# An attention-and-feed-forward layer on one core: query, key and value projections in nine 64-row blocks instead of five 128-row ones

## The chip, the core and the metric

The kernel runs on one core of one Trainium2 chip. The metric is device time in microseconds (us). Three runs of the kernel before the change took 446.04, 446.70 and 447.26 us; their median is 446.7 us. Profiles come from one execution each. A difference below about 0.3% (1.3 us) can't be told from no change here.

## What is computed

x has 2048 tokens of 576 features, in bf16. The attention cuts the tokens into four segments of 512. Within a segment it is ordinary causal attention with 32 heads of 18 features; across segments a memory matrix M and a vector z are carried on. A feed-forward of width 4608 follows.

```python
q, k, v = ln(x) @ wq, ln(x) @ wk, ln(x) @ wv          # 576 x 576 each
for s in range(4):                                    # segments of 512 tokens
    a_dot = softmax(qs @ ks.T * scale + causal mask) @ vs
    a_mem = phi(qs) @ M / (phi(qs) @ z + 1e-6)        # phi(t) = t + 1 if t > 0 else exp(t)
    o = g * a_mem + (1 - g) * a_dot
    M, z = M + phi(ks).T @ vs, z + sum(phi(ks))
h   = x + o @ wo
out = h + gelu(ln(h) @ w1 + b1) @ w2 + b2             # 576 -> 4608 -> 576
```

## The kernel before

The work is cut by segment and, inside one, by tile of 128 tokens. `stage_X` (line 752) normalizes the four x tiles of a segment and brings them into `xreg` with the features on the partitions. `stage_P` (line 845) multiplies them by wk, wq and wv, tile by tile. `stage_A0` and `stage_A` (lines 969 and 1104) do the attention of segment 0 and of segments 1 to 3, `stage_M` (line 915) updates the memory, `stage_B` (line 1224) multiplies by wo, adds x and normalizes again, and `stage_C` (line 1273) does the feed-forward: first product at lines 1337 (segment 0) and 1300, second at 1387.

**Projections.** 576 features are four blocks of 128 rows and one of 64. x is stored 640 wide: its last 64 features stand twice, so that the fifth block holds them in both halves of the partitions. The weights of the fifth block have the 64 rows in the upper half for the first 288 output columns and in the lower half for the others, and zeros elsewhere. One projection of one tile has three forms:

- `proj2` (line 830, matmuls at 837): 10 matmuls over all 128 rows. k and q of the first two tiles of segment 0 use it.
- `proj_pair` fused (line 823): also 10 matmuls over 128 rows, five for each of the two PSUM banks.
- `proj_pair` in two pieces (line 797): 18 matmuls over 64 rows, two at a time in the two halves of the array, 10 in the first piece and 8 in the second. Each half of the rows writes one bank in the first piece and the other bank in the second. Between them VectorE or GpSimd does a tiny memset (`pass`, line 803), which the second piece waits for.

The output projection with wo uses `proj_pair` as well. The first product of the feed-forward (lines 1300 and 1337) has a form of its own: nine blocks of 64 rows, each half of the array with its own bank from beginning to end, and a `by_pair` layout of the weights that gives the two halves the nine blocks in different orders.

**Turning x.** In segment 0 five TensorE transposes a tile (`TX`, line 747) fill a PSUM bank, and one copy on ScalarE or VectorE (lines 643 and 647) takes all five blocks into `xreg`. In segments 1 to 3 the tiles are stored to DRAM (`xnd`), and one transposing DMA for each pair of tiles (line 634, queue of SyncE) brings five blocks of 256 columns back.

**Start.** Eight matmuls on zeros (`warm_up`, line 657) and two more (line 661) run while the first x tile arrives. Its first half comes over SyncE's queue, its second half and the whole second tile over ScalarE's queue (lines 685 and 687); the two halves of the k weights follow on SyncE's queue. Three more zero matmuls stand behind the first tile's transposes, and the first projection waits for them.

**Buffers.** `xreg` has 19 blocks of 512 columns: two slots of five for x, and two of nine for the feed-forward's input, one of which lies over the first. PSUM is eight banks; a score takes four (`st`), a projection two. `t1` (two buffers) holds the values after the transposition of a group's result from PSUM (lines 1047 and 1196) until `comb` (1056) or `comb2` (1207) has read them. Five `pt` tiles hold exponentiated scores.

**Order.** Nothing is scheduled by the hardware or by a framework. `TIMETABLE` gives each operation a rank and an engine; `Graph.schedule` sorts by rank and emits each engine's instructions in that order. Each engine works through its own list strictly in order, so an instruction that waits holds up all behind it.

The functions that the change touches, and what calls them:

Of the kernel before, what the change touches and what calls it, by code (L numbers as in the profile page):

```python
# [13 lines left out]
F32 = mybir.dt.float32  # L14
BF16 = mybir.dt.bfloat16
# [458 lines left out]
def kernel(  # L474
# [11 lines left out]
    nc = tc.nc  # L486
# [1062 lines left out]
```

## Time and profile before

| | |
|---|---|
| runs | 446.04, 446.70, 447.26 us, median 446.7 |
| profiled execution | 446.14 us; span from first to last instruction 444.4 us |
| granted TensorE clock | 1.000 |
| TensorE busy | 433.7 us (98%) |
| VectorE, ScalarE, GpSimd busy | 286.3, 298.1, 179.5 us |
| DMA | 76.26 MB, 63.5% of 16 engines' time on the main queue |

How to read it: a matmul's end is modelled in the profile and covers its way through the array, so neighbouring matmuls overlap. Start-to-start distances and merged pieces of the chain say more than the mean of one. The chain of waits is the sequence of work that ended last, followed back from the end; where it runs through one engine without a break, that engine sets the time.

### The profile page before, as it was taken

To read this page: it belongs to the slowest core of one execution; us is meant where nothing else is said; L and a number is where in the kernel's file an instruction comes from. 1 tells how busy PE (TensorE), PEld (TensorE's weight loads), DVE (VectorE), ACT (ScalarE), POOL (GpSimd) and SP (SyncE) were. 2 spreads that over 40 slices of the span, in tenths; PEclk is the share of its full clock that TensorE was granted. 3 is DMA by queue.
4 is the path that set the end of the run, shared out by engine and by line. 5 is a ranking of instruction groups with operands and counts; after the bars stand their busy time and mean duration, and the time that the engine had idled before them with its cause. 6 is when DMAs were issued, how large, how long until landed. Compare 5 with 4: busy or idle time off the path is not lost.

```text
span 444.4 us, 12086 instructions
## 1 busy us (share of the span) xinstructions
PE 433.7 (98%) x5089; PEld 277.8 (63%) x5089; DVE 286.3 (64%) x635; ACT 298.1 (67%) x274; POOL 179.5 (40%) x321
## 2 busy tenths in 40 slices
PE   8978999999999999999999999999999999999997
PEld 4755677776677676664444766654457775446775
DVE  4899988899778998968788888642875410000011
ACT  3799889999878898776799976675855001565000
POOL 4587657356735765834132765412111400110000
DMA  7599989997999955893783236913634357550110
GB/s 283 167 217 258 257 251 283 251 287 203 191 270 333 286 118 175 175 236 94 162 228 91 73 90 193 232 20 133 219 97 165 90 142 133 172 177 1 40 41 29
DMA packets 81591, 76.26 MB, mean 172 GB/s; under 512 B 59008, under 2 KB 68864, under 8 KB 81536
## 3 DMA queue, kind: packets, MB, share of 16 engines
q1 hardware_dynamic: 81248, 75.23, 63.5%
q8 instruction: 40, 0.66, 0.6%
q10 hardware_dynamic: 288, 0.25, 0.2%
q14 instruction: 15, 0.12, 0.1%
HBM read 42.30 MB, written 19.20 MB: 138 GB/s over the span
## 4 chain that ended last, share of the span: by engine, by line
PE 87%; DVE 5%; ACT 4%; DMA 2%; issue 1%; ACTq 0%; SPq 0%; DVEq 0%
PE bank L1387 32%; PE bank L1300 24%; PE bank L1337 7%; PE bank L797 6%; PE bank L823 5%; PE bank L1162 4%; PE bank L1188 3%; ACT pt L1166 1%; PE bank L837 1%; DMA x<-in_A_x_dram 1%; DMA beta_bc<-in_A_beta_dram 1%; PE bank L1133 1%; PE bank L1001 1%; ACT pt L1004 1%; DVE pt L1014 1%
## 5 line engine op out<-in xcount | busy, mean ns | idle before, releaser
L1166 ACT ACTIVATE pt<-bank 128x2048 bf16<-128x2048 f32 x60 | 112.6, 1876 | 29.5 <-PE bank L1162 23.2
L1387 PEld LDWEIGHTS <-hT 128*128 128x128 bf16 x1152 | 110.2, 98 | 34.5 <-issue 6.7
L1300 PE MATMUL bank<-xreg,w1g 64*128 64x512 bf16 x972 | 108.0, 376 | 0.0
L1300 PEld LDWEIGHTS <-w1g 64*128 64x128 bf16 x972 | 46.5, 94 | 57.4 <-issue 3.7
L1387 PE MATMUL bank<-w_lo,hT 128*128 128x288 bf16 x576 | 78.1, 286 | 0.0
L1387 PE MATMUL bank<-w,hT 128*128 128x288 bf16 x576 | 77.4, 286 | 0.0
L1399 DVE TENSOR_TENSOR ot<-bank,hc 128x288 bf16<-128x288 f32 x32 | 13.8, 448 | 88.4 <-PE bank L1387 72.5
L1177 POOL TENSOR_SCALAR_AFFINE_SELECT pt<-pt 128x512 bf16<-128x512 bf16 x64 | 45.0, 717 | 42.5 <-ACT pt L1166 41.6
L1305 ACT ACTIVATE hT<-bank,b_col 128x512 bf16<-128x512 f32 x36 | 22.2, 695 | 46.5 <-PE bank L1300 46.3
L1315 DVE TENSOR_SCALAR hT<-bank,b_col 128x512 bf16<-128x512 f32 x46 | 32.8, 741 | 22.1 <-PE bank L1300 20.4
L1373 POOL TENSOR_TENSOR hc<-hc,b_bc 128x576 f32<-128x576 f32 x9 | 11.8, 1320 | 79.0 <-DMA hc<-hd 79.0
L1004 ACT ACTIVATE pt<-bank 128x2048 bf16<-128x2048 f32 x20 | 37.4, 1876 | 4.1 <-PE bank L1001 2.9
L1337 PE MATMUL bank<-xreg,w1g 64*128 64x256 bf16 x648 | 38.1, 269 | 0.0
L823 PE MATMUL bank<-hT,xreg 128*128 128x288 bf16 x250 | 33.8, 286 | 1.7 <-ACT pt L1004 1.0
L1337 PEld LDWEIGHTS <-w1g 64*128 64x128 bf16 x648 | 30.4, 94 | 6.6 <-issue 3.2
L1320 ACT ACTIVATE hT<-hT 128x8192 bf16<-128x8192 bf16 (+2 forms) x6 | 31.8, 5323 | 0.1
L823 PEld LDWEIGHTS <-xreg 128*128 128x128 bf16 x250 | 23.4, 98 | 10.0 <-issue 4.3
L1313 ACT ACTIVATE hT<-bank,b_col 128x512 bf16<-128x512 f32 x26 | 16.9, 685 | 16.1 <-PE bank L1300 15.8
L797 PE MATMUL bank<-hT,xreg 64*128 64x288 bf16 x342 | 24.9, 283 | 0.9 <-DVE qk_pad L647 0.7
L1204 POOL TENSOR_TENSOR t<-t,r 128x288 f32<-128x288 f32 x17 | 13.6, 802 | 29.2 <-DVE r L1201 29.2
L1348 DVE TENSOR_TENSOR hT<-bank,b_col 128x512 bf16<-128x512 f32 x31 | 20.4, 682 | 6.0 <-PE bank L1337 5.8
L1162 PE MATMUL bank<-qk 32*128 32x512 bf16 (+3 forms) x384 | 23.8, 301 | 0.2
(120 smaller groups left out, 592.1 us busy)
## 6 DMA issues: line engine op xcount, KB each, us to landing
w1g<-in_B_w_dram SPq DMA_DIRECT2D x41, 576.0 KB, 5.0
qkd<-qk_pad SPq DMA_DIRECT2D x15, 512.0 KB, 4.8
hd<-h SPq DMA_DIRECT2D x16, 288.0 KB, 3.6
hc<-hd SPq DMA_DIRECT2D x16, 288.0 KB, 3.6
w_lo<-in_B_w_dram SPq DMA_DIRECT2D x3, 864.0 KB, 7.0
w<-in_B_w_dram SPq DMA_DIRECT2D x3, 864.0 KB, 7.5
xb<-in_A_x_dram SPq DMA_DIRECT2D x16, 144.0 KB, 3.1
x2d<-xn SPq DMA_DIRECT2D x14, 160.0 KB, 1.9
```

The source lines that it names most:

```text
L797: return nc.tensor.matmul(out=cc[hf].t[:, 0:HALF], lhsT=xTb.t[r, k, ts], rhs=wt[r, hf, k, :], start=start, stop=stop, skip_group_check=True)
L823: nc.tensor.matmul(out=cc[hf].t[:, 0:HALF], lhsT=xTb.t[:, k, ts], rhs=wt[:, hf, k, :], start=(k == 0), stop=(k == KT - 1))
L1004: ex = add(ps, {"act": 1.88}, lambda e: nc.scalar.activation(out=pt.t[:], in_=st.t[:], func=ACT.Exp, scale=scale), [sc], pt, [st], table=" ...
L1162: nc.tensor.matmul(out=st.t[:, i, off:off + n_], lhsT=qk[rows, 1, kt * P:(kt + 1) * P], rhs=qk[rows, 0, kt * P:L], start=True, stop=True, ...
L1166: ex = add(ps, {"act": 1.88}, lambda e, st=st, pt=pt: nc.scalar.activation(out=pt.t[:], in_=st.t[:], func=ACT.Exp, scale=scale), [sc], pt, ...
L1177: nc.gpsimd.affine_select(out=blk, in_=blk, pattern=[[0, 4], [1, P]], compare_op=ALU.is_ge, fill=0.0, base=0, channel_multiplier=-1)
L1300: nc.tensor.matmul(out=cc[w].t[:], lhsT=w1.t[rows, k, q, :], rhs=x2T[s].t[rows, k, :], start=(k == 0), stop=(k == ND - 1))
L1305: ready_f[f + w] = [add(pf - 12, {"act": 0.68}, lambda e, f=f, w=w, cc=cc: nc.scalar.activation(out=hT[:, :, f + w, :], in_=cc[w].t[:].rea ...
L1315: nc.vector.tensor_scalar(out=dst, in0=src, scalar1=b, scalar2=None, op0=ALU.add)
L1320: ge = add(2.9, {"act": 0.42 * (f1 - f0) + 0.2}, lambda e, f0=f0, f1=f1: nc.scalar.activation(out=hT[:, :, f0:f1, :], in_=hT[:, :, f0:f1, ...
L1337: nc.tensor.matmul(out=cc[w].t[:, q * 2 * P:(q + 1) * 2 * P], lhsT=w1.t[rows, k, q, :], rhs=x2T[s].t[rows, k, ts], start=(k == 0), stop=(k ...
L1387: nc.tensor.matmul(out=c.t[:, 0:HALF], lhsT=hT[:, tl // 2, f, (tl % 2) * P:(tl % 2 + 1) * P], rhs=w2_c[ch][:, f - ch * WCH, hf * HALF:(hf ...
```

## The change

- The input is doubled over both halves of the partitions. x is stored with its **first** 64 features again at the end; nine blocks of 128 rows then hold feature chunks of 64 as (0,1), (2,3), (4,5), (6,7), (8,0) ("even") and (1,2), (3,4), (5,6), (7,8) ("odd").
- `proj9` takes the place of `proj2` and of `proj_pair` for q, k and v: 18 matmuls over 64 rows, two at a time, each half of the array with a bank of its own, no pass. Only k of the first tile is in two parts (five blocks, then four), so that it can begin with the even blocks and the first part of the weights. `proj_pair` stays for wo.
- Each turned tile gets nine blocks instead of five: with TensorE four more transposes and a second copy, with DMA a second transposing DMA of four blocks.
- The first two tiles of segment 1 are turned by TensorE instead of by DMA; stores and turns of that half over DRAM go.
- The second x tile moves from ScalarE's queue to SyncE's, between the first tile and the k weights. The q, k and v weights are 9/10 as large.
- Of the zero matmuls at the start 8 of 512 columns and 1 of 256 are left (before 13 of 512); the projection doesn't wait for them.
- `xreg` is 45 blocks of 256 columns: three half-segment slots of nine for x. To make room `t1` has one buffer instead of two, and `MZacc` lies where the last of the second product's weights come later.
- `TIMETABLE` is new for all operations: order and engine of most of them change.

```diff
-    xreg = const.tile([P, 2 * KT + ND, L], BF16, name="xreg")
-    xT_s = Slots([xreg[:, j * KT:(j + 1) * KT, :] for j in range(2)])
+    xreg = const.tile([P, 5 * ND, 2 * P], BF16, name="xreg")
+    xT_s = Slots([xreg[:, j * ND:(j + 1) * ND, :] for j in range(3)])
...
-    t1_s = slots(2, [P, 16, 32], "t1", F32)
+    t1_s = slots(1, [P, 16, 32], "t1", F32)
...
-        x1 = add(-7.8, {"act": 0.45}, lambda e: nc.scalar.dma_start(out=x0.t[:, 1, :], in_=x[P:2 * P, :]), [x0b], None, [x0], name="x1")
+        x1 = add(-7.8, {"sp": 0.45}, lambda e: nc.sync.dma_start(out=x0.t[:, 1, :], in_=x[P:2 * P, :]), (), None, [x0], size=254e3, name="x1")
+        x1.behind = x0b
...
+                even = transposes(prio + 0.1 * tl, xn, [ap], lambda buf=buf, j=j: buf.t[:, 0:KT, j * P:(j + 1) * P],
+                                  None if j else buf, [buf] if j else [], name="TX", one=0.06 if s or tl else 0.108)
+                odd = transposes(prio + 0.1 * tl, xn, [ap], lambda buf=buf, j=j: buf.t[:, KT:ND, j * P:(j + 1) * P], None, [buf], ND - KT, name="TX", c0=64, one=0.06 if s or tl else 0.108)
...
+                    prev = flip(prio + 0.3, lambda buf=buf: buf.t[:, 0:KT, :], lambda j=j: xnd[s][j * 2 * P:(j + 1) * 2 * P, :], 400e3,
+                                [wr[2 * j], wr[2 * j + 1]], acq=buf, cost=1.8)
...
+                    odd = flip(prio + 0.3, lambda buf=buf: buf.t[:, KT:ND, :], lambda j=j: xnd[s][j * 2 * P:(j + 1) * 2 * P, 64:D], 320e3,
+                               [prev.after], use=[buf], cost=1.5)
...
+        def proj9(prio, xTb, tl, nm, after, c, cc, parts):
+            ts = slice(tl % 2 * P, (tl % 2 + 1) * P)
+            wt, prev, own = wts[nm], None, [c] if c else cc
+
+            def fn(e, k0, k1):
+                for k in range(k0, k1):
+                    for w in range(2):
+                        r = slice(64 * w, 64 * w + 64)
+                        out = c.t[:, w, 0:HALF] if c else cc[w].t[:, 0:HALF]
+                        nc.tensor.matmul(out=out, lhsT=xTb.t[r, k, ts], rhs=wt[r, k, :], start=(k == 0), stop=(k == ND - 1))
...
-        PE_FLIP_O, PE_FLIP_X, DMA_FLIP_X, PE_QK = (0,), (0,), (1, 2, 3), (0, 1)
+        PE_FLIP_X, PE_X, PE_QK = (0,), ((0, 0), (0, 1), (1, 0)), (0, 1)
...
+    sides = ([0, 2, 4, 6, 8, 1, 3, 5, 7], [1, 3, 5, 7, 0, 2, 4, 6, 8])
...
-        A_x=np.concatenate([a["A_x"], a["A_x"][:, :, 512:]], axis=2),
+        A_x=np.concatenate([a["A_x"], a["A_x"][:, :, :64]], axis=2),
```

More of the change, by code (lines that the diff above doesn't have):

```diff
@@ L411, in schedule @@
         free = dict.fromkeys(ENGINES, 0.8)
-        table, dma, flying, done = {}, 0.0, [], set()
+        table, dma, flying, done = {"act": "exp"}, 0.0, [], set()
         order = sorted(self.ops, key=lambda o: o.start)
@@ L453, in schedule @@
             free[e] = max(t0, op.end - OVER.get(e, 0.0))
+            op.end += op.lat
             if e == "sp":
@@ L561 @@
     tri = const.tile([P, P], BF16, name="tri")
-    MZacc = const.tile([P, G, 76], F32, name="MZacc")
     MZ_blk = [const.tile([P, G, P], BF16, name=f"MZ_blk{j}") for j in range(2)]
@@ L586 @@
     xn_s = slots(3, [P, XW], "xn", pool=over)
+    MZacc = over.tile([P, G, 76], F32, name="MZacc")
     def to_w2():
@@ L660, in build @@
         wprev = warm_up(4, 1.72, [wprev], [Buf(c_s), Buf(c_s)])
-        wprev = add(-9, {"pe": 0.5}, lambda e: [nc.tensor.matmul(out=wst.t[:], lhsT=warm[:, 0:P], rhs=warm[:], start=True, stop=True) for _ in range(2)],
-                    [wprev], wst, name="warm")
+        add(-9, {"pe": 0.22}, lambda e: nc.tensor.matmul(out=wst.t[:, 0:2 * P], lhsT=warm[:, 0:P], rhs=warm[:, 0:2 * P], start=True, stop=True),
+            [wprev], wst, name="warm")
         half_ok = memset(-9, "dve", 0.1, mhalf[:], val=-0.5)
@@ L736, in layernorm, with transposes @@
             return add(prio, {"dve": dcost}, apply, [a, b if centred is None else None] + list(extra), dst_buf, [sm, xsrc], name="apply")
-        xnT, xn_ok, applied, begun = {}, {}, [], []
-        def transposes(prio, buf_src, after, dst, dbuf_acq, dbuf_use, nk=KT, name="T", c0=0):
+        xnT, xn_ok, applied = {}, {}, []
+        def transposes(prio, buf_src, after, dst, dbuf_acq, dbuf_use, nk=KT, name="T", c0=0, one=0.06):
             c = Buf(c_s)
@@ L747, in fn @@
                     nc.tensor.transpose(out=ptv[:, k * P:(k + 1) * P], in_=buf_src.t[:, c0 + k * P:c0 + (k + 1) * P], identity=ident[:])
-            a = add(prio, {"pe": 0.06 * nk}, fn, list(after) + [ident_ok], c, [buf_src], name=name)
+            a = add(prio, {"pe": one * nk}, fn, list(after) + [ident_ok], c, [buf_src], name=name)
             return copy(prio - 0.5, 0.70 if nk == KT else 0.60, 0.50 if nk == KT else 0.42, dst, lambda: c.t[:].bitcast(BF16)[:, 0:nk * P].rearrange("p (k q) -> p k q", q=P), [a],
@@ L774, in stage_X @@
                     continue
[L775 to L784 removed]
+                buf, j = bufs[tl // 2], tl % 2
@@ new lines, in stage_X @@
+                even = transposes(prio + 0.1 * tl, xn, [ap], lambda buf=buf, j=j: buf.t[:, 0:KT, j * P:(j + 1) * P],
+                                  None if j else buf, [buf] if j else [], name="TX", one=0.06 if s or tl else 0.108)
+                odd = transposes(prio + 0.1 * tl, xn, [ap], lambda buf=buf, j=j: buf.t[:, KT:ND, j * P:(j + 1) * P], None, [buf], ND - KT, name="TX", c0=64, one=0.06 if s or tl else 0.108)
+                odd.after.append(even)
+                if j:
+                    even.after.append(xn_ok[s, tl - 1][0])
@@ L785, in stage_X @@
+                xn_ok[s, tl] = [even, odd]
+            prev = None
+            for j in range(2):
+                if (s, j) not in PE_X:
                     first = prev
-                    prev = flip(prio + 0.3, lambda j=j: buf.t[:, :, j * 2 * P:(j + 1) * 2 * P], lambda j=j: xnd[s][j * 2 * P:(j + 1) * 2 * P, :], 400e3,
-                                wr[2 * j:2 * j + 2], acq=None if j else buf, use=[buf] if j else [], cost=1.8)
+                    buf = bufs[j]
+                    prev = flip(prio + 0.3, lambda buf=buf: buf.t[:, 0:KT, :], lambda j=j: xnd[s][j * 2 * P:(j + 1) * 2 * P, :], 400e3,
+                                [wr[2 * j], wr[2 * j + 1]], acq=buf, cost=1.8)
@@ L828, in proj_pair @@
             return b
-        def proj2(prio, xTb, tl, nm, after, c):
-            ts = slice(tl * P, (tl + 1) * P)
-            wt = wts[nm]
-            def fn(e):
-                for hf in range(2):
-                    for k in range(KT):
-                        nc.tensor.matmul(out=c.t[:, hf, 0:HALF], lhsT=xTb.t[:, k, ts], rhs=wt[:, hf, k, :],
-                                         start=(k == 0), stop=(k == 4))
-            return add(prio, {"pe": 1.24}, fn, list(after) + w_ok[nm], c, [xTb], name="P" + nm)
+        def proj9(prio, xTb, tl, nm, after, c, cc, parts):
[7 more added lines that the diff above has]
+                        nc.tensor.matmul(out=out, lhsT=xTb.t[r, k, ts], rhs=wt[r, k, :], start=(k == 0), stop=(k == ND - 1))
+            for n, (k0, k1) in enumerate(parts):
+                todo = list(after) if len(parts) == 1 else list(after)[n:n + 1] + list(after)[2:]
+                prev = add(prio, {"pe": round(0.1225 * (k1 - k0) + 0.003, 4)}, lambda e, k0=k0, k1=k1: fn(e, k0, k1), todo + [prev] + (w_ok[nm] if len(parts) == 1 else w_ok[nm][n:n + 1]),
+                           None if n else own, [xTb] + (own if n else []), table="rows64", name="PR"[n] + nm)
+            return prev
         fk_bufs, v_ok, qk_st, v0_read, mz_read = {}, {}, {}, [], {}
@@ L1492, in _layout @@
     a = {k: np.asarray(v) for k, v in inputs.items()}
+    sides = ([0, 2, 4, 6, 8, 1, 3, 5, 7], [1, 3, 5, 7, 0, 2, 4, 6, 8])
     def blocks(w):
-        w5 = np.zeros((128, 5, 2, 288), w.dtype)
-        w5[:, 0:4] = w[0:512].reshape(4, 128, 2, 288).transpose(1, 0, 2, 3)
-        for h in range(2):
-            w5[64 * h:64 * h + 64, 4, h] = w[512:576].reshape(64, 2, 288)[:, h]
-        return w5
+        c = w.reshape(9, 64, 2, 288)
+        w9 = np.concatenate([c[order, :, h].transpose(1, 0, 2) for h, order in enumerate(sides)]).reshape(128, -1)
+        return np.concatenate([w9, np.zeros((128, 288), w.dtype)], axis=1)
     w1, b1 = a["B_w1"], a["B_b1"]
@@ L1504, in by_pair @@
         c = w.reshape(9, 64, 9, 2, 2, 128)
-        return np.concatenate([c[order, :, :, :, h].transpose(2, 1, 0, 3, 4) for h, order in enumerate(
-            ([0, 2, 4, 6, 8, 1, 3, 5, 7], [1, 3, 5, 7, 0, 2, 4, 6, 8]))], axis=1).reshape(9 * 128, 9 * 256)
+        return np.concatenate([c[order, :, :, :, h].transpose(2, 1, 0, 3, 4) for h, order in enumerate(sides)], axis=1).reshape(9 * 128, 9 * 256)
     def by_quadrant(w):
```

58 lines of the change are left out of this document (27 added, 31 removed), and 599 rows, old and new, of the table TIMETABLE.

## The prediction

> **What bounds the kernel now.** I read the page first, then PE's waits, then the chain in order of time.
>
> ```profile
> span 444.4 us, 12086 instructions
> ...
> PE 87%; DVE 5%; ACT 4%; DMA 2%; issue 1%; ACTq 0%; SPq 0%; DVEq 0%
> ```
>
> TensorE is the bound for most of the span. The list of what PE waited for, from 45.3 us to the end, has two rows:
>
> ```profile
> PE bank L823 <- DVE MZacc L937: 0.3, 1, 0.3
> PE bank L797 <- DVE qk_pad L647: 0.2, 1, 0.2
> ```
>
> So after 45.3 us PE stands still for 0.5 us in all. There only less PE work can help, and a new order can hardly wait less. Ahead of that it is different. Busy time in stretches of 10 us (PE, PEld, DVE, ACT, POOL, clock, DMA share, GB/s):
>
> ```profile
> 0.00:10.00 10.00, 8.05 (x40) 4.23 (x41) 4.76 (x15) 3.23 (x5) 3.47 (x13) 1.00 0.78 281
> ...
> 20.00:30.00 10.00, 7.57 (x136) 5.42 (x136) 9.24 (x23) 9.92 (x15) 7.98 (x15) 1.00 0.95 170
> 30.00:40.00 10.00, 8.27 (x179) 5.15 (x171) 9.77 (x24) 8.75 (x11) 7.41 (x15) 1.00 1.12 253
> 40.00:50.00 10.00, 9.03 (x118) 6.05 (x119) 9.82 (x26) 8.55 (x9) 7.63 (x17) 1.00 0.93 273
> ```
>
> From 20 to 45 us VectorE has 9.2 to 9.8 busy us in 10, ScalarE 8.6 to 9.9, and PE has gaps of 1.0 to 2.4. The 5% of the chain that are VectorE's lie here. One row of the chain, in order of time, is the point to which all this leads:
>
> ```profile
> 45.33 2.82 PE bank L823 x20
> ```
>
> At 45.33 us stands the first output projection (wo), from which PE no longer waits. I split the sum there: **when** it comes, and **how much** PE work is left behind it.
>
> **The change part by part. 1: PE work behind that point.** Merged pieces of the chain in which groups of projections follow each other, and the counts behind 45.3 us:
>
> ```profile
> 88.22 2.56 PE bank L823 x20
> ...
> 106.08 2.31 PE bank L797 x36
> ```
> ```profile
> L823 PE MATMUL bank<-hT,xreg 128*128 128x288 bf16 x150 | 20.1, 286 | 0.0
> L797 PE MATMUL bank<-hT,xreg 64*128 64x288 bf16 x270 | 18.9, 283 | 0.2 <-DVE qk_pad L647 0.2
> ```
>
> A fused projection costs 2.56 / 2 = 1.28 us, one in 64-row pairs 2.31 / 2 = 1.155 us: nine slots instead of ten. The new form is the second without its pass, so I price it at 1.155. Behind 45.3 us stand 150 / 10 = 15 fused and 270 / 18 = 15 in pairs. The 15 fused give 15 x 0.125 = 1.9 us. Of the others one waits 0.2 us at its pass. The instruction order, as built, has one fused wo projection more (40 matmuls instead of 30): 0.1 us back. Changes between full, 64-row and 32-row matmuls behind the first wo projection are 183 instead of 182: nothing. It also shows 18 q, k, v groups ahead of the first wo projection in both kernels, and all added transposes ahead of it. **Behind it: -1.9 - 0.2 + 0.1 = -2.0 us**, with ends -1.5 (groups at 1.18, with their own changes of mode) and -2.5.
>
> **2: the start.** What the second x tile holds up:
>
> ```profile
> 3.02 0.82 DVE L719 BATCH_NORM_STATS2 ln<-x 128x6 f32<-128x288 bf16 x2 [1.83 <-DMA x<-in_A_x_dram]
> ...
> 6.09 0.82 DVE L719 BATCH_NORM_STATS2 ln<-x 128x6 f32<-128x288 bf16 x2 [1.37 <-DMA x<-in_A_x_dram]
> ```
> ```profile
> 7.63 0.45 PE L747 MATMUL bank<-ident,xn 128*128 128x128 bf16 x5 [0.70 <-DVE xn L733]
> 7.92 5.06 PE L837 MATMUL bank<-hT,xreg 128*128 128x288 bf16 x40
> ```
>
> The first x piece is in at 3.0 us. The 160 KB of the second tile, straight behind it at 281 GB/s, need 0.6 us and are in by 3.7, before VectorE is done with tile 0 (6.09 - 1.37 = 4.72). VectorE gains the 1.37 us. Tile 1 is then transposed at 7.63 - 1.4 = 6.2 us, nine transposes and a copy on either engine longer, and k begins near 7 us instead of 7.92: **-1.0**. The k weights come 160 KB later but are a tenth smaller: 72 + 88 + 160 + 648 KB at 281 GB/s are 3.5 us behind the first transfer, 5.7 us, so they don't hold k up. ScalarE's queue loses an issue and SyncE's gets one of about 0.45 us; the loads behind it wait for the first x tile anyway.
>
> ```profile
> 16.82 0.40 PE L1001 MATMUL bank<-qk 32*128 32x128 bf16 x16
> ```
> ```profile
> 18.59 0.23 ACT L1440 ACTIVATE g_bc<-beta_bc 128x32 f32<-128x32 bf16 x1 [0.97 <-DMA beta_bc<-in_A_beta_dram]
> 18.73 1.86 ACT L1004 ACTIVATE pt<-bank 128x2048 bf16<-128x2048 f32 x1
> ```
>
> The first score is done by about 17.2 us, but its exp waits until 18.73 behind evictions and behind the load of beta. In the new order the exp is ahead of beta's: up to 1.5 us more on ScalarE, so -1.0 to -2.5 there.
>
> **3: the added evictions ahead of the wo projection.** Groups of the first 45 us:
>
> ```profile
> L1014 DVE TENSOR_TENSOR pt<-pt,tri 128x1024 bf16<-128x1024 bf16 x3 | 3.8, 1268 | 0.0
> ...
> L647 DVE COPY xreg<-bank 128x640 bf16<-128x640 bf16 x3 | 1.5, 492 | 0.7 <-PE bank L747 0.5
> ```
> ```profile
> L643 ACT COPY qk<-bank 128x1024 bf16<-128x1024 bf16 x2 | 1.9, 1015 | 0.0
> ...
> L643 ACT COPY xreg<-bank 128x640 bf16<-128x640 bf16 x1 | 0.7, 692 | 2.6 <-PE bank L747 2.6
> ```
>
> Twelve copies into `xreg` replace four, six on each engine. A four-block copy I take at 4/5 to all of a five-block one: VectorE +3 at 0.39 to 0.49, about +1.3; ScalarE +5 at 0.55 to 0.69, +3.2. One copy of q and k (1.0 us on ScalarE; on VectorE not seen, estimated 1.2) changes sides. Two masks of 1.27 us go from VectorE to GpSimd, which has room (7.4 of 10 us). The passes that fall away here I cost at nothing; each comes between two pieces of a projection, and only one held PE up behind this stage. VectorE: +1.3 + 1.2 - 2.5 = 0; ScalarE: +3.2 - 1.0 = +2.2, and a few evictions more. Against the gains of part 2 (VectorE -1.4, ScalarE -2.5) VectorE comes out 1.4 early and ScalarE about even. PE has 34 transposes more; at the row L747 above five are 0.45 us, so they are some 3 us, in stretches where PE has 1.0 to 2.4 us of gaps in each 10. I take the wo projection **1.0 us earlier**, nearer to VectorE's side because VectorE is in the chain; ends 2.6 earlier (VectorE's 1.4, and the copy of 1.2 in time that it has free before 20 us) and 1.5 later (ScalarE's 3.2 us all on the path, with half of the start's gain).
>
> **4: DMA.** Five transposing DMAs of four blocks are added, one of five goes, with two stores.
>
> ```profile
> xreg<-xnd SPq DMA_TRANSPOSE x6, 4.9
> ```
>
> Each takes 4.9 us to land beside others, in a time when the engines are 93 to 112% busy. I cost it at nothing, since PE waits for no DMA behind 45.3 us. If that cover were gone, a projection that comes to stand at its odd blocks would wait up to one landing, 4.9 us, once; other groups are there to fill most of it, and I take +1 as the upper end. The Trainium skill, "DMA: Bandwidth & Descriptors", section "Latency and other measured facts", gives 261 GB/s for a transposing DMA: 262 KB would be 1.0 us each, an estimate of 4 us of DMA time in all, and by it the sum would be the same.
>
> **5: a new order's own waits.** The order is new for every operation and the old one has only 0.5 us of waits to lose. I add **+0.4 us**, between 0 and the 4 us that the slower rival below reaches.
>
> **Sum.** 446.1 (profiled execution; its span is 444.4, the rest lies around it) - 2.0 - 1.0 + 0.4 = **443.5 us**. That execution was 0.6 us under the median of the runs, inside their spread of 1.2.
>
> **Rivals.** *a) The evictions eat the start.* ScalarE, at 9.92 of 10 us from 20 to 30, carries five copies more; the wo projection comes 1.5 us late: 446.1 + 1.5 - 2.0 + 0.4 = 446.0. For it: ScalarE's row; against it: the early exp.
>
> *b) One t1 buffer makes it slower.* The rows that a group's chain is made of:
>
> ```profile
> L1196 DVE STREAM_TRANSPOSE t<-bank x24: 653/705/718, 100.7 to 315.4; 128x512 f32<-128x512 f32 x24
> ...
> L1204 POOL TENSOR_TENSOR t<-t,r x17: 671/746/1205, 102.5 to 320.8; 128x288 f32<-128x288 f32 x17
> ...
> L1207 POOL TENSOR_TENSOR o_nat<-t,t x14: 806/812/1247, 107.5 to 322.4; 128x288 bf16<-128x288 f32 x14
> ```
>
> From the transposition to the last read at least 0.7 + 0.75 + 0.8 = 2.25 us pass, over two engines. With one buffer VectorE stands at the next transposition until GpSimd is done; behind it are PSUM evictions that PE's next group waits for, and the value's bank and `pt` tiles stay held. For 24 chains in the 220 us there is room on average, and the new order spreads them; against it that they bunch in segment 1. If a quarter us a chain reached PE, that would be 24 x 0.25 = 6 us: 449.5. It is slower than before from (446.1 - 443.5) / 24 = 0.11 us a chain.
>
> *c) TensorE stays slow for longer at the start.*
>
> ```profile
> 1.25 3.59 PE L657 MATMUL bank<-pt 128*128 128x512 bf16 x8 [1.25 <-DVE mhalf L623]
> ...
> 6.02 0.91 PE L657 MATMUL bank<-pt 128*128 128x512 bf16 x3
> ```
>
> Eight zero matmuls take 3.59 us, about 0.43 each; three of the same at 6.02 take 0.91 with the way out of the array. The full rate comes in between the two, near 6.2 us, although the granted clock reads 1.00 throughout. With fewer zero matmuls and gaps near 5 and 6 us the array may get there only during k and q: three groups at half rate are 3 x 1.155 us, half of it in time that PE would have waited: +1.7, so 445.2. The Trainium skill, "TensorE: Matmul & The Clock Gate", section "Part 1: The HAM clock gate", says that the array starts at half clock and is released after some 3.4 us of sustained work in a free-running window; this rule speaks for c; the trace, with 5 us from the first matmul, agrees in kind.
>
> *d) More comes of the start.* VectorE is the only bound up to the wo projection and gets the 2.6 us: 441.9 or a little less.
>
> That the second tile isn't earlier at all, because both queues share the engines, ends in a.
>
> **How the numbers follow.** Forecast (442.3 to 444.7) 0.48; d (to 440) 0.16; c 0.08; a 0.13; b 0.15. What a measurement can tell is 0.3% of 446.7, 1.3 us: faster means below 445.4. Forecast, d and c lie there: 0.72. Case a and the weak half of b are within 0.3%: 0.15; b beyond 448.0: 0.13. The range leaves out the upper part of b and a little below d: 440.0 to 448.2.
>
> **What would show it.** Right: stats of tile 1 without a DMA wait; k from about 7 us; the wo projection near 44.3; two projections that follow each other in 2.31 us or less; PE's waits behind it under 1 us. Wrong: the wo projection after 46 us with ScalarE full ahead of it (a); `t` or `o_nat` as releaser of VectorE's transposition, and PE waiting behind 100 us (b); 0.25 us between the first projection's pairs (c).

## The result, and the profile after

The changed kernel takes 447.81 us (median of 22 runs, 445.88 to 449.75), the kernel before 445.99 us on the same chips (22 runs, 445.35 to 447.26). The ratio is 1.0040, 95% interval 1.0028 to 1.0052: **slower by 0.4%**, where the prediction said faster by 0.6%. The runs of the changed kernel also spread over 3.9 us, twice as far as those of before (1.9). With 22 runs of each the interval is about 0.12% to either side, finer than the 0.3% that three runs allowed.

The profiled execution took 446.46 us and so is one of the quick ones of its kernel. The page of the changed kernel, its span and its chain by engine:

```profile
span 444.7 us, 12623 instructions
...
PE 75%; DVE 7%; DMA 6%; ACT 6%; POOL 2%; issue 2%; SPq 1%; POOLq 0%; DVEq 0%; ACTq 0%
```

Before, the chain had 87% on PE. The 12 points are now the DMAs', VectorE's, ScalarE's and GpSimd's. When does the first wo projection come, and how quick are two projections behind each other? Pieces of the chain in order of time:

```profile
42.02 2.31 PE bank L835 x36
44.66 2.56 PE bank L819 x20
```

Two projections take 2.31 us, as predicted, and the wo projection stands at 44.66 instead of 45.33 us: 0.67 us earlier. From there to the end of the span it was 444.4 - 45.33 = 399.1 us and is now 444.7 - 44.66 = 400.0. So the predicted 2 us less are gone and 0.9 us has come on top. The saving itself is there: PE is busy for 393.1 us of this stretch, where it was 395.6. What PE waited for behind 44.5 us (in total, times, longest), where the same list of before had 0.5 us:

```profile
PE bank L1134 <- DVE t L1197: 0.8, 1, 0.8
PE bank L835 <- DVE qk_pad L634: 0.6, 1, 0.6
PE bank L1338 <- DMA w1g<-in_B_w_dram: 0.6, 1, 0.6
PE bank L1189 <- DVE v_aug L634: 0.5, 1, 0.5
PE bank L1189 <- DVE t L1143: 0.4, 1, 0.4
PE bank L1189 <- POOL pt L1178: 0.3, 1, 0.3
PE bank L1189 <- DVE pt L1176: 0.2, 1, 0.2
PE bank L1301 <- DMA w1g<-in_B_w_dram: 0.2, 1, 0.2
```

Eight waits, 3.6 us: 3.1 more than before. With -2.0 us of work that is +1.1, and the stretch grew by 0.9. Three of the waits lie between 103 and 109 us and name VectorE. The stretches 100 to 110 and 110 to 120 us of the kernel before (PE, PEld, DVE, ACT, POOL, clock, DMA share, GB/s):

```profile
100.00:110.00 10.00, 9.94 (x150) 6.34 (x150) 9.07 (x25) 9.80 (x13) 5.98 (x12) 1.00 0.72 192
110.00:120.00 10.00, 9.81 (x129) 6.59 (x126) 7.11 (x20) 8.90 (x12) 7.54 (x13) 1.00 0.93 206
```

and of the changed one:

```profile
100.00:110.00 10.00, 8.13 (x136) 5.16 (x134) 9.46 (x21) 9.50 (x11) 8.58 (x14) 1.00 1.01 236
110.00:120.00 10.00, 10.00 (x172) 6.89 (x168) 9.89 (x21) 8.52 (x13) 6.84 (x9) 1.00 1.11 240
```

VectorE's 9.07 + 7.11 busy us have become 9.46 + 9.89, 3.2 us more, and PE has 1.9 us of gaps in the first stretch. The chain of the changed kernel there shows how:

```profile
99.95 0.46 DVE qk_pad L634
100.40 0.73 DVE ln L710 x2
...
102.09 0.58 POOL ln L715
102.67 0.03 issue
102.70 0.89 DVE xn L726
...
104.01 0.46 DVE v_aug L634
104.47 0.04 issue
104.52 0.72 PE bank L1189 x16
```

The values at 104.52 need a PSUM bank. By the profile it is freed by the eviction of `v_aug` at 104.01, which has the end of a layernorm ahead of it in VectorE's order (`xn`, 102.70), and that one waits for two small operations of GpSimd.

### The profile page after: what moved, and what is told of

Same layout as the page of the kernel before. It is cut to its first block, busy times and chain, and to the rows that moved or that the text cites. A ratio compares the mean times of both kernels' runs of the same rounds, so it can differ in the third digit from the quotient of the medians.

```text
span 444.7 us, 12623 instructions
## 1 busy us (share of the span) xinstructions
PE 431.7 (97%) x5355; PEld 278.3 (63%) x5355; DVE 291.2 (65%) x636; ACT 296.7 (67%) x269; POOL 179.3 (40%) x312
## 4 chain that ended last, share of the span: by engine, by line
PE 75%; DVE 7%; DMA 6%; ACT 6%; POOL 2%; issue 2%; SPq 1%; POOLq 0%; DVEq 0%; ACTq 0%
PE bank L1388 27%; PE bank L1301 21%; PE bank L835 9%; PE bank L1338 6%; DMA w1g<-in_B_w_dram 4%; PE bank L1163 3%; ACT hT L1355 3%; PE bank L1189 3%; PE bank L793 2%; DMA x<-in_A_x_dram 2%; ACT pt L1167 1%; PE bank L1002 1%; PE bank L819 1%; DVE ln L710 1%; POOL pt L1178 1%
## 5 line engine op out<-in xcount | busy, mean ns | idle before, releaser
L1388 PE MATMUL bank<-w,hT 128*128 128x288 bf16 x576 | 78.3, 286 | 0.0
L835 PE MATMUL bank<-hT,xreg 64*128 64x288 bf16 x864 | 58.0, 283 | 1.1 <-DVE qk_pad L634 0.6
L1306 ACT ACTIVATE hT<-bank,b_col 128x512 bf16<-128x512 f32 x36 | 22.5, 689 | 46.0 <-PE bank L1301 46.0
L1178 POOL TENSOR_SCALAR_AFFINE_SELECT pt<-pt 128x512 bf16<-128x512 bf16 x58 | 42.0, 737 | 27.1 <-ACT pt L1167 26.9
L835 PEld LDWEIGHTS <-xreg 64*128 64x128 bf16 x864 | 41.6, 94 | 14.3 <-issue 5.0
L1316 DVE TENSOR_SCALAR hT<-bank,b_col 128x512 bf16<-128x512 f32 x49 | 34.9, 742 | 18.6 <-PE bank L1301 18.5
L1374 DVE TENSOR_TENSOR hc<-hc,b_bc 128x576 f32<-128x576 f32 x7 | 5.6, 817 | 43.8 <-DMA hc<-hd 43.8
L1314 ACT ACTIVATE hT<-bank,b_col 128x512 bf16<-128x512 f32 x23 | 15.1, 685 | 21.9 <-PE bank L1301 21.6
L1176 DVE TENSOR_TENSOR pt<-pt,tri 128x512 bf16<-128x512 bf16 x38 | 21.5, 569 | 4.7 <-ACT pt L1167 4.7
```

What stands on the lines that cost most here:

```text
L835: nc.tensor.matmul(out=out, lhsT=xTb.t[r, k, ts], rhs=wt[r, k, :], start=(k == 0), stop=(k == ND - 1))
L1176: nc.vector.tensor_tensor(out=blk, in0=blk, in1=tri[:].unsqueeze(1).to_broadcast([P, 4, P]), op=ALU.mult)
L1178: nc.gpsimd.affine_select(out=blk, in_=blk, pattern=[[0, 4], [1, P]], compare_op=ALU.is_ge, fill=0.0, base=0, channel_multiplier=-1)
L1306: ready_f[f + w] = [add(pf - 12, {"act": 0.68}, lambda e, f=f, w=w, cc=cc: nc.scalar.activation(out=hT[:, :, f + w, :], in_=cc[w].t[:].rea ...
L1316: nc.vector.tensor_scalar(out=dst, in0=src, scalar1=b, scalar2=None, op0=ALU.add)
L1388: nc.tensor.matmul(out=c.t[:, 0:HALF], lhsT=hT[:, tl // 2, f, (tl % 2) * P:(tl % 2 + 1) * P], rhs=w2_c[ch][:, f - ch * WCH, hf * HALF:(hf ...
```

## The experiments

Theory **A**: the new order's own waits, above all VectorE filled where TensorE's evictions come due. Rivals: **B**, the one `t1` buffer; **C**, the five added transposing DMAs; **D**, the start, where the second x tile ahead of the k weights only moves a wait. All ratios are to the kernel before, run beside each (445.75 to 445.99 us).

| run | edit | median us | ratio, 95% |
|---|---|---|---|
| changed | | 447.81 | 1.0040 (1.0028 to 1.0052) |
| e1 | two `t1` | 447.44 | 1.0035 (1.0022 to 1.0048) |
| e2 | no odd transposing DMAs | 446.46 | 1.0012 (1.0003 to 1.0020) |
| e3 | no two tails | 446.78 | 1.0023 (1.0011 to 1.0035) |
| e4 | before, x1 first | 446.05 | 1.0004 (0.9995 to 1.0013) |
| e5 | before's order | 462.40 | 1.0362 (1.0340 to 1.0384) |
| e6 | q weights first | 451.32 | 1.0116 (1.0087 to 1.0145) |
| e7 | w1g loads first | 447.20 | 1.0032 (1.0018 to 1.0046) |
| e8 | changed, second profile | 447.69 | one run |
| e9 | e2 and e3 | 446.46 | 1.0014 (1.0004 to 1.0024) |
| e10 | x1 back on ScalarE's queue | 447.55 | 1.0037 (1.0023 to 1.0052) |
| e11 | layernorm ends later | 447.67 | 1.0048 (1.0031 to 1.0064) |
| e12 | e11, e7 and four exchanges | 447.97 | 1.0051 (1.0037 to 1.0065) |
| e13 | VectorE's work to GpSimd | 446.30 | 1.0010 (0.9998 to 1.0022) |
| e14 | e13 and two exchanges | 445.73 | 0.9994 (0.9984 to 1.0005) |
| e15 | no odd DMA in segment 1 | 447.01 | 1.0026 (1.0015 to 1.0037) |
| e16 | e14 and e2 | 444.57 | 0.9973 (0.9963 to 0.9983) |
| e17 | e14, three more moves | 446.30 | 1.0014 (1.0005 to 1.0023) |
| e18 | e17, two transpositions later | 446.88 | 1.0027 (1.0014 to 1.0040) |

### Four causes, one at a time (e1 to e4)

```diff
-    t1_s = slots(1, [P, 16, 32], "t1", F32)
+    t1a_s, t1_s = Slots([t1_t, t1_hc]), Slots([t1_t, t1_x])
```

> The changed kernel with two buffers t1 again (the second lies in memory that is idle by then: x in segments 1 to 3, hc in segment 0); the order of every engine is unchanged. Changed kernel: 447.8 us (445.9 to 449.8). Theory A (the new order's own waits: evictions and DMA turns that come due together; about 6.3 us of PE stalls behind the first wo projection): no change, 447.3 to 448.3, and the stalls near 103.8, 106.5 and 108 us stay. Theory B (one buffer t1 serializes VectorE's transpositions of the values): 2 to 4 us less, 444 to 446, and the stalls shrink by as much.

The interval overlaps the changed kernel's almost wholly, and the list of waits has VectorE's rows between 103 and 109 us with the same numbers, 0.8 us at line 1134 (here 1137) among them. **B falls.** (The 6.3 us of stalls in this expectation are more than the 3.6 of the list.)

```diff
                     odd.behind = prev
+                    odd.fn = lambda e: None
```

> The changed kernel without the transposing DMAs of the odd halves in segments 1 to 3: the projections there read what an earlier segment left in those rows. Leaves out those DMAs and nothing else. Theory A (the order's own waits): 447.0 to 448.0, at most the waits for w1g (0.8 us by the profile's list) go. Theory C (the added transposing DMAs take SyncE's queue and the DMA engines from other loads and cause the stalls and the wider spread): 1.5 to 4 us less, 444 to 446.3, with a spread like that of before (under 2 us).

1.35 us less, and the 11 runs lie within 0.9 us (446.13 to 447.04). That is just beyond C's own time, but the spread is C's, and A's forecast (447.0 or more) missed. VectorE's waits stand unchanged in its list; those for w1g are gone, and one of 0.9 us for `hT` has come (e7 and e8 return to it). So the DMAs cost something of their own. The stretch from 80 to 100 us of the changed kernel:

```profile
80.00:100.00 20.00, 19.93 (x365) 14.39 (x359) 18.66 (x46) 19.91 (x16) 9.09 (x18) 1.00 1.01 225
```

and of e2:

```profile
80.00:100.00 20.00, 19.93 (x363) 14.28 (x361) 18.66 (x46) 19.91 (x17) 9.35 (x18) 1.00 0.75 202
```

PE, VectorE and ScalarE do the same work to a hundredth; only the share of the DMA engines falls, from full to three quarters.

```diff
+                if (s, tl) in ((0, 2), (0, 3)):
+                    ap.fn = lambda e: None
```

> The changed kernel without the two copies of 64 columns behind the layernorms of x2 tiles 2 and 3 of segment 0 (VectorE, 0.49 and 0.67 us at 103.6 and 105.1 us); part of those two tiles' transposed halves is then stale. Theory A (VectorE, filled between 100 and 110 us, releases TensorE too late): about as much less as is taken out, 0.8 to 1.3 us, so 446.5 to 447.0, and the stalls of 0.8, 0.6 and 0.5 us there shrink. Theories B and C: no change, 447.8.

1.0 us less in the median, but with an interval that overlaps the changed kernel's: inconclusive. e9 tries it again.

```diff
-        x1 = add(-7.8, {"act": 0.45}, lambda e: nc.scalar.dma_start(...
+        x1 = add(-7.8, {"sp": 0.45}, lambda e: nc.sync.dma_start(...
-    "x1": "a 10",
+    "x1": "s 8.5",
```

> The kernel before with only the second x tile moved from ScalarE's queue to SyncE's, ahead of the k weights. Before: 446.0 us. The prediction's step for the start: first projection 0.5 to 1 us earlier, scores up to 1.5 us earlier, time 445.0 to 445.6. Rival (k weights land later by what x1 takes, and TensorE has enough other work behind the start that nothing is left): 446.0 to 446.6.

The rival's time: nothing that can be measured is gained. In e4's profile k begins at 6.83 instead of 7.92 us, but then

```profile
9.91 2.61 PE L838 MATMUL bank<-hT,xreg 128*128 128x288 bf16 x20 [0.47 <-DMA hT<-in_A_w_dram]
```

q waits for its weights until 9.91. Before, q followed k without a wait, at 7.92 + 5.06 / 2 = 10.4. Half of the gain is gone there, and nothing measurable is left at the end.

### The order, the start and one wait (e5 to e8)

e5 has the changed kernel's work and two `t1` buffers in the order of the kernel before; only what the new parts force was moved (`x1` on SyncE's queue, copies and transpositions at the places of the old ones, one block on the memory ahead of the w2 loads).

> The changed kernel's work (doubled x, nine blocks, half of segment 1 turned on TensorE, x1 on SyncE) with the order of the kernel before, moved only where the new parts have to stand, and with two buffers t1. Before 446.0 us, changed 447.8. Theory A (the edits are worth what TensorE's work says, the new order's waits eat it): 442 to 444.5, stalls behind the first wo projection under 3 us. Theory C (the added transposing DMAs cost the time in any order): 446 to 448, with stalls on w1g, qk and w_lo loads. If it is near 445.5 to 446.5 without stalls on DMAs, other engines than TensorE bound the kernel and the saved work was not worth its time in any order.

It can't answer its question, because the adaptation makes troubles of its own. Its first wo projection comes at 49.41 us, 4.1 us later than before, and far from the edits there is a long wait:

```profile
PE bank L1183 <- POOL pt L1172: 3.6, 1, 3.6
PE bank L1382 <- DMA w<-in_B_w_dram: 1.3, 1, 1.3
```

The mask that PE waits for (line 1172) stands in GpSimd's order behind the block on the memory. The chain has that block at 155.8 to 157.9 us, right behind the product at 155.3 us that reads the buffer which it writes; by the kernel's order the w2 loads come after it too. What holds for the edits in the old order stays open.

```diff
-    "X00dma": "s 16 24 14",
+    "X00dma": "s 14 24 16",
```

> The changed kernel with the q weights issued ahead of the fourth x tile instead of behind it (one exchange on SyncE's queue at 3.5 us). In two of four profiles of kernels with this start TensorE waits 0.7 to 0.8 us for the q weights at 9.2 us. Theory D (the second x tile ahead of the k weights only moves the wait from k to q; the wider spread of the changed kernel comes from there): 0.5 to 1 us less, 446.8 to 447.3, and a narrower spread. Theory C (transposing DMAs behind 33 us make the spread): no change, 447.8.

Slower by 3.5 us, with a spread of 5.2 (448.20 to 453.37). The profile is of the quickest execution, only 0.4 us above the changed kernel's median. In it the q weights hold up the third x tile: VectorE waits 2.45 us for it until 9.25 us, where the changed kernel waits 0.45 until 7.26. PE's list up to 44.5 us has a row that the changed kernel has at 0.2 us at most:

```profile
PE bank L738 <- DVE xn L726: 1.6, 1, 1.6
```

The other five executions had a mean granted clock of 0.992 to 0.996, where the profiled one had 1.000 and the changed kernel's 22 had 0.999 or 1.000. Over some 446 us, 0.4 to 0.8% are 1.8 to 3.6 us, an estimate: a lower clock can be most of the loss. Which wait lowers it, no profile shows. So D's remedy doesn't help: what goes ahead makes something else late.

```diff
-    "A2flip": "s 706 668 818 843 819 888 967 1037",
+    "A2flip": "s 743.5 668 818 843 819 888 967 1037",
```

> The changed kernel with one transposing load of q and k (the one that waits on SyncE's queue from 127.4 to 132.4 us) moved behind the three w1g and w2 loads that follow it. Theory A: the wait of 0.82 us at 139.2 us goes, 447.0 to 447.3. If other engines bound that stretch, or the moved load is late instead: 447.8 or more.

Not told apart from the changed kernel. In the profile the wait for w1g at 139 us is gone, and another stands behind it, 0.9 us for `hT` ahead of the values at 144.66 us (the first row of e8's list below). The one had covered the other.

> The changed kernel, unchanged, for a second profile: its first is one of its quickest executions (446.46 us, median 447.8). Theory D: an execution near the median shows the first wo projection about 1 us later than 44.6 us, behind waits for the q weights or the w_lo loads, and the same stalls behind it. Theory A alone: the same start and longer stalls between 100 and 140 us.

447.69 us, near the median, with the wo projection at 44.64 us as before: the start is not what makes this execution longer. Behind it the list has 4.5 us instead of 3.6. The new row is the one for `hT`, and the two waits for w1g have the same sum, but the first lies near 77 us instead of 139:

```profile
PE bank L1189 <- DVE hT L1349: 0.9, 1, 0.9
PE bank L1134 <- DVE t L1197: 0.8, 1, 0.8
...
PE bank L1338 <- DMA w1g<-in_B_w_dram: 0.4, 1, 0.4
...
PE bank L1301 <- DMA w1g<-in_B_w_dram: 0.4, 1, 0.4
```

Which loads land late differs from execution to execution.

That doesn't rule D out for other executions. In the profiles of e1 (448.19 us), e3 (447.44) and e11 (449.91) PE waits 0.7 to 0.9 us for the q weights near 10 us, and the first wo projection comes at 45.95, 45.31 and 45.21 us. The edits of e3 and e11 lie behind 100 us and can't have moved it. So the start itself varies by 0.7 us and more between executions, and is a part of the spread.

### Do the causes add up, and is it VectorE's order or its load (e9 to e13)

e9 has the edits of e2 and e3 together.

> The changed kernel without the odd transposing DMAs of segments 1 to 3 and without the two tails (both leave-outs at once; those projections and part of two transposed x2 tiles then read stale data). Alone they took 1.35 and 1.0 us off 447.8. Theory A+C (two causes beside each other: VectorE filled at 100 to 110 us, and DMAs that land late): the sum, 445.2 to 445.7, under the 446.0 of before. If both act through the same waits: 446.2 to 446.5.

The same as e2 alone, the time expected if both act through the same waits. The lists say otherwise: in e3 and e9 the rows for `t` (0.8 us) and `v_aug` (0.5) are gone, in e2 those for w1g. But little of what goes is gained. From the first wo projection to the values near 144.5 us e9 takes 99.9 us and e2 100.2. So beside e2's edit the tails are worth some 0.2 us, and the rest of e3's 1.0 us stays within its interval.

e10 puts `x1` back on ScalarE's queue, the reverse of e4's diff.

> The changed kernel with the second x tile back on ScalarE's queue, where the kernel before has it. The prediction's step for the start: 0.5 to 1 us more, 448.3 to 448.8. Theory D (x1 ahead only moves the wait from the k to the q weights, which land near 9.2 to 10 us either way, as e4 showed for the kernel before): no change or less, 447.0 to 448.0, with a spread no wider than the changed kernel's.

No change that can be measured, in either direction. Together with e4: **the order of these two loads is worth nothing that these runs can tell.** The first wo projection stands at 44.84 us in e10, as early as with the second x tile ahead.

```diff
-    "B02apply": "d 556",     "B02tail": "d 557",     "B03apply": "d 543",     "B03tail": "d 550",
+    "B02apply": "d 595.5",   "B02tail": "d 596",     "B03apply": "d 582",     "B03tail": "d 582.5",
-    "P2fk": "d 477 502 567 605",
+    "P2fk": "d 477 502 577.5 605",
```

(The two stores behind the tails move to ranks 611 and 612.)

> The changed kernel with ranks moved and nothing left out: the two layernorm ends of x2 tiles 2 and 3 (apply and tail, 2.7 us of VectorE from 102.7 to 105.7 us) and one fk (1.07 us) stand behind the evictions and transpositions that TensorE waits for. Theory A: the stalls of 0.68 and 1.0 us at 103.8 and 106.5 us go and part of 0.82 us at 108, 446.0 to 446.8. If VectorE's load alone counts, not its order, the stalls come back at 109 to 117 us: 447.5 or more.

The second case. In e11, whose profile is of its slowest execution (449.91 us),

```profile
100.00:110.00 10.00, 9.62 (x155) 5.96 (x151) 7.27 (x19) 9.68 (x12) 8.20 (x14) 1.00 1.12 234
110.00:120.00 10.00, 8.22 (x128) 5.78 (x126) 9.87 (x20) 7.49 (x11) 6.26 (x8) 1.00 0.51 161
```

PE's gap has gone from the first stretch (8.13 to 9.62) and come back in the second (10.00 to 8.22), where VectorE now has 9.87. The work that was put off falls on evictions there: **in this order the wait has only moved.** That no other order would do is not shown. VectorE stands idle for 2.07 us until 106.59 us in e11, room that this order doesn't fill. e12 says the same of single places: it is e11 with e7's move and four exchanges.

> As e11, and also: the waiting load of q and k behind the w1g loads (e7), one addition behind two evictions at 144 us, one score ahead of the values at 136 us, one hc addition behind a transposition at 185 us, one product with the memory ahead of values at 270 us. Theory A: the stalls of 0.5 to 1.1 us at these places go too, 444.3 to 445.5, under before by up to 1.7 us. If a wait that goes is followed by the next one close behind it (as in e7): 446 to 447.

The waits at 185 and 270 us are gone from its list and one of 1.1 us for an exponential has come at 137, from the score that was put ahead of the values.

```profile
PE bank L1163 <- ACT pt L1167: 1.5, 3, 1.1
```

e13 leaves the places and takes load off VectorE:

```diff
-    "B02tail": "d 557",
+    "B02tail": "g557",
-    "B03tail": "d 550",
+    "B03tail": "g550",
-    "M1mblk": "g 560",
+    "M1mblk": "g 633.5",
```

and, in the same way, masks 10 and 11 (ranks 572 and 602) and the second `comb` (581) of segment 1 from `d` to `g`.

> The changed kernel with five operations between 103 and 113 us moved from VectorE to GpSimd (two tails, two masks, one scaling of values: about 3.5 us of VectorE) and GpSimd's 2.7 us block on the memory moved from 106 us to its idle time at 116 us. Nothing left out. Theory A' (VectorE's load from 84 to 122 us bounds that stretch, whatever its order): the stalls of 2.5 us at 103.8 to 108 shrink to under 1 and do not come back before 122 us; 446.0 to 446.8. If the wait only moves to GpSimd or to loads: 447.5 or more, with stalls that name POOL or DMA.

1.5 us less, by an interval that lies wholly under the changed kernel's. Its stretches, and the one row of its list that lies in them:

```profile
100.00:110.00 10.00, 9.26 (x147) 6.11 (x145) 8.88 (x20) 9.53 (x11) 8.64 (x15) 1.00 1.08 222
110.00:120.00 10.00, 10.00 (x174) 6.86 (x170) 9.54 (x19) 8.96 (x13) 9.75 (x15) 1.00 1.07 262
```

```profile
PE bank L834 <- DVE qk_pad L633: 0.3, 1, 0.3
```

Of the three waits at 103 to 108 us (0.8, 0.6 and 0.5) 0.3 is left, PE has 1.1 us more to show in the first stretch, and none of it is given back in the second. GpSimd is now the full one (9.75). **A holds in this form: load taken off VectorE in that stretch shortens the kernel.** The run also puts GpSimd's block on the memory (`M1mblk`) later, to make room; what that does by itself was not tried.

### What is left (e14 to e18)

e14 is e13 with two of e12's exchanges: `D01hc` from `d940` to `d963`, behind a transposition, and `A3val`'s fourth entry from 1312 to 1313.5, behind a product with the memory (one tail on GpSimd goes from 1308 to 1311.5 with it).

> As e13, with the two exchanges of e12 that took the stalls at 185 us (one hc addition behind a transposition) and 270 us (one product with the memory ahead of values) away, each 0.6 us there. If these stalls lie on the path: 1.2 us less than e13, 444.8 to 445.8. If not: as e13.

445.73 us, the kernel before's time. The step from e13, 0.6 us, is half of what was expected and not told apart by the intervals; the step from the changed kernel, 2.1 us, is. Nothing is left out in e14. Its list has 2.7 us, of which the longest is

```profile
PE bank L1337 <- DMA w1g<-in_B_w_dram: 1.1, 1, 1.1
```

e15 is e2's edit for segment 1 alone.

> The changed kernel without the odd transposing DMA of segment 1 alone, the one that is issued near 35 us between the loads of q and k; the projections of half of segment 1 read stale data. Without all five such DMAs the time was 446.5 us with a spread of 0.9 us. Theory C1 (this one, among the loads that the start waits for, makes the spread): 446.5 to 446.9, spread under 2 us. Theory C2 (the later four, ahead of the w1g loads that TensorE waits for at 76.6 us): 447.4 to 447.8, spread as before.

In the middle between C1 and C2, and told apart from neither the changed kernel nor e2: inconclusive.

> As e14, and without the odd transposing DMAs of segments 1 to 3 (projections read stale data there). If the causes stand beside each other: e14 less 1.0 to 1.4 us, 443.6 to 444.6, near the predicted 443.5. If the DMAs' waits lie beside the others: as e14.

e16 has e14's ranks and e2's edit: 444.57 us, 1.2 less than e14 by intervals that don't touch, and less than before by 0.27% (0.17 to 0.37%). So e13's load off VectorE, e14's exchanges and the DMAs add up: 1.5, 0.6 and 1.2 are, unrounded, 3.2 of the 4.3 us between 447.8 and the predicted 443.5. The list of e16 has 1.8 us left, with the 1.1 us for w1g gone:

```profile
PE bank L1189 <- DVE hT L1349: 0.9, 1, 0.9
PE bank L1301 <- DMA w1g<-in_B_w_dram: 0.4, 1, 0.4
PE bank L835 <- DVE qk_pad L633: 0.3, 1, 0.3
PE bank L1189 <- DVE pt L1176: 0.2, 1, 0.2
```

e17 is e14 with `C00dma`'s entries 380, 386, 387 at 345, 353.5, 382.5, `C01copy`'s 759 and 760 at 751.2 and 751.4, and one mask from 712 to 709.5.

> As e14, nothing left out, with three more ranks moved: three w1g loads ahead of loads that wait on SyncE's queue at 58 to 63 us (the wait for w1g at 76.6 us is 0 to 1.3 us by the profile), two evictions ahead of a mask and an addition at 143 us (wait of 1.07 us), one mask ahead of an eviction at 135 us (0.5 us). If these waits lie on the path: 0.8 to 1.6 us less than e14's 445.7, 444.1 to 444.9, and faster than before by 0.2 to 0.4%. If the next wait takes their place, as in e7 and e12: 445.5 to 446.

Slower than e14 by 0.6 us, with intervals that barely touch. The waits for w1g and for `hT` ahead of the values are gone, and others have come. One is for the transposing loads of q and k, which now stand behind w1g on SyncE's queue:

```profile
PE bank L1162 <- DVE hT L1348: 0.7, 1, 0.7
...
PE bank L1162 <- DMA qk<-qkd: 0.5, 1, 0.5
```

This profile is of e17's quickest execution (445.32 us), so it doesn't show what makes the median one longer.

> As e17, and two of the added transpositions of segment 1 on TensorE stand behind the scores that they stand ahead of (TensorE waits 1.07 and 0.74 us at 26.8 and 29.8 us for their evictions before it may write those scores). If the added evictions hold up the start: first wo projection 0.5 to 1.5 us earlier, 443 to 444.4. If ScalarE's exponentials bound the start instead: as e17.

446.88 us (`X1TX` "142 147.5 154 164.5", its copies after them): no gain either, the same row of qk at 1.0 us, and a first wo projection that is no earlier (44.94 us, in e17 44.13). No version of mine with all of the work beats the kernel before; e14 equals it.

## Why the prediction was wrong

**Step 5, "a new order's own waits: +0.4", failed, and with it the reading that it rests on, "There only less PE work can help".** The list of PE's waits has 3.6 us in a quick execution and 4.5 in one near the median, against 0.5 before: +3.1 to +4.0, at the upper end of the 0 to 4 us that the step allowed. The reasoning was wrong, not just the size. It takes a PE without waits as the only bound, so that saved work comes off the time and a new order can cost next to nothing. The rows of the kernel before show otherwise. In 100 to 110 us VectorE had 9.07 and ScalarE 9.80 busy us of 10, and the 25 us ahead of that have ScalarE at 24.80:

```profile
75.00:100.00 25.00, 24.87 (x392) 18.65 (x392) 22.77 (x54) 24.80 (x19) 11.96 (x23) 1.00 1.09 278
```

The chain behind 45.3 us, too, leaves PE there:

```profile
101.05 1.89 ACT pt L1166
...
103.76 1.88 ACT pt L1166
...
108.75 0.80 DVE qk_pad L647 x2
109.55 0.62 DVE t L1142
...
110.44 0.89 DVE xn L735
111.32 1.10 DVE hc L1373
```

Between 74 and 113 us 13.3 us of it are ScalarE's and 3.9 VectorE's, so the prediction's reading that VectorE's part of the chain lies ahead of 45 us holds for most of it only. PE was barely the last here, and matmul work saved in such a stretch has the same evictions to wait for. On top of that the new order put 3.2 us more of VectorE's work between 100 and 120 us. Some of it taken off brought 1.5 us back (e13). What the saving alone would have met in the old order is not shown (e5). The sum used busy time by stretches only up to 50 us.

**Step 4, "I cost it at nothing, since PE waits for no DMA behind 45.3 us", failed too**: 1.2 us (e16 against e14) to 1.35 us (e2), just above its +1. That the DMAs were no wait of the old kernel said nothing of one with five more in a time when the engines are full. What the profiles show of the price is other loads that land late (w1g near 77, 139 and 392 us). The lists of e8 and e14 have 0.8 and 1.3 us for w1g (4.5 and 2.7 us in all), those of e2 and e16 none and 0.4 (3.7 and 1.8). The Trainium skill, "DMA: Bandwidth & Descriptors", section "Latency and other measured facts", gives 261 GB/s for a transposing DMA, by which the five would be some 5 us of DMA time, an estimate. No run here times one alone. Nor is the wide spread of the runs shown to be these DMAs': e2 without them spreads over 0.9 us but e9, also without them, over 2.0, and e17 with them over 1.7.

**Steps 2 and 3, the start: -1.0.** Measured 0.67 in the first profile, and in others of the same start anything from nothing (45.31 us in e3) to 1.1 (44.19 in e14). The mechanism was not right either: tile 1's stats did come without a DMA wait (4.69 us) and k began at 7.64 (6.9 to 7.6 in other profiles), yet x1 ahead of the k weights is worth nothing that can be measured (e4, e10). "The k weights come later but don't hold k up" left out q's weights behind them. What brings the wo projection forward was not tried apart.

**Step 1, -2.0, was right or a little small**: two projections take 2.31 us, and 399.1 us behind the wo projection less 2.0, plus 3.1 of new waits, is 400.2, against 400.0 seen. By PE's busy time in these stretches the saving is 2.5 us, the far end of the step's range; the list of waits leaves out the shortest ones.

The sum for the profiled execution, with what was measured: 446.1 - 2.0 - 0.7 + 3.1 = 446.5 (446.46). With the two inexact terms just named, that it meets the time to a tenth is partly luck. The median lies 1.35 us above it: e8 shows 0.9 more in waits.

Of the **rivals**, a did not come (the wo projection is early in most profiles) nor c (k and q of the first tiles, 72 matmuls, take 4.58 us, 0.127 a pair). b was the one with the right sign and nearly the right place, "behind 100 us", and the wrong cause: with two buffers nothing changes (e1). Its argument, that VectorE standing still holds the evictions that PE's next group waits for, was right for the layernorm's end at 102.7 us.

**Open**: why e16 still lacks 1.1 us of the forecast (its list has 1.8 us of waits, and the start's gain is smaller than counted); what the edits would be worth in the old order, or in one that puts no more on VectorE there (e5); which of the five DMAs cost most (e15); what makes the changed kernel's runs spread, besides the start and the loads.

## What to carry to other kernels

Before pricing saved TensorE work, read the chain and the busy time of the evicting engines in the very stretch where the work is saved, and what a new order adds to them there. Few waits of TensorE don't show that it has room to finish sooner: here it had 0.5 us, beside engines at 9 to 9.8 of 10 us. In this kernel a stall that named VectorE shrank when load was taken off VectorE in that stretch (e13); putting its work later, or clearing one wait, mostly brought the next (e7, e11, e12, e17). Added loads on full DMA engines were paid by others' landing times (e2, e16).

## What the runs showed of the hardware

One long wait seems to have cost e5 more than itself. In e5 PE waits 3.6 us at 155.7 us and then (the granted clock is the column behind POOL)

```profile
155.00:160.00 5.00, 1.43 (x15) 0.64 (x16) 2.03 (x5) 1.46 (x2) 3.94 (x7) 0.82 0.21 42
160.00:165.00 5.00, 4.08 (x28) 2.06 (x21) 3.94 (x8) 1.88 (x1) 4.81 (x8) 0.50 1.01 352
165.00:170.00 5.00, 4.63 (x28) 2.68 (x27) 0.42 (x2) 2.28 (x2) 0.83 (x2) 0.66 0.92 280
```

the granted clock is 0.82, 0.50 and 0.66 over 15 us, though PE is busy again for 82 and 93% of the last two stretches; a wait of 1.3 us for w lies in them. The Trainium skill, "TensorE: Matmul & The Clock Gate", section "HAM oscillation — how this bites in real kernels", puts the point at idle gaps of more than about 3.4 us, and here the trace agrees. But in this case it is no lower bound: e5 also has

```profile
30.00:40.00 10.00, 8.00 (x174) 5.88 (x161) 6.88 (x13) 9.07 (x10) 7.89 (x15) 0.83 0.97 249
```

behind several waits of 1.4 us or less, while the profiled executions of the changed kernel and e6, with single waits of up to 1.8 us at the start, keep the full clock throughout. Five other executions of e6 don't (0.992 to 0.996 in the mean, and 2.0 to 5.2 us longer). What decides below 3.6 us these runs don't show.
